# RMSNorm over 16,384 rows: other store sizes, and eight small memsets on VectorE

## Chip, cores and metric

The kernel runs on one core of one Trainium2 chip. The metric is the device time of one execution in microseconds (us); lower is better. The kernel before has a median of 105.37 us over 6 runs (105.22 to 106.1).

## The reference

```python
B, S, D = 512, 32, 640          # x is bf16 [512, 32, 640], g is bf16 [640]
def reference(x, g):
    rms = jnp.sqrt((x * x).mean(axis=-1, keepdims=True) + 1e-6)
    return x / rms * g
```

Each of the 512 x 32 = 16,384 rows of 640 numbers is divided by its root mean square and multiplied by the vector g. The input is 20.97 MB and the output is as large, so 41.9 MB have to move between HBM and SBUF.

## The kernel before

**Layout.** The 16,384 rows are spread over 128 partitions, 128 consecutive rows on each. In what follows "row" means one of these 128 positions: one row is 128 partitions x 640 numbers, or 160 KB. The whole input is kept in SBUF in one tile, `xs`; the result is written over it in place, and stored from there. There are no buffers to wait for on the way in or out.

**Three lists of sizes**, each adding up to 128 rows, cut the work:

- `LOADS = [4, 8, 8, 16, 32, 32, 28]`: seven loads, issued one after the other by ScalarE's queue at the start (L72). The fifth brings rows 36 to 67, the sixth rows 68 to 99, the seventh rows 100 to 127. In each load a partition's rows are one contiguous run.
- `CHUNKS = [2, 2] + [8] * 15 + [4]`: 18 chunks of compute. They end after rows 2, 4, 12, 20, 28, 36, 44 and so on up to 124 and 128.
- `STORES = [28, 24, 24, 24, 8, 8, 8, 4]`: eight stores, issued by SyncE (SP, L139). A store is put into SP's program as soon as all its rows belong to finished chunks, and it waits for VectorE's write of the last of its rows.

**One chunk.** TensorE copies each row of the chunk into PSUM by a multiplication with the identity (`ident`, L108), in two pieces of 512 and 128 columns. ScalarE squares it there and sums it up (L110), one row at a time, into `ms`. (The first chunk of two rows does this on VectorE instead, L99.) ScalarE then takes the square root for the chunk (L119, `rstd`). VectorE multiplies the chunk by g (`times_g`, L124, into `y`), takes the reciprocal (L128), and multiplies each row of `y` by its own factor, one instruction per row, into `xs` (`finish`, L130).

**The order.** The order on PE, VectorE, SP and GpSimd is that in which the code stands (a manual schedule). The loop is pipelined by one chunk: `times_g` of chunk c comes ahead of `finish` of chunk c-1. So VectorE needs the rows of a chunk, loaded, before it finishes the chunk before it; and SP issues a store only after `finish`.

At the start VectorE sets two constants: `ones1` (L64), used to broadcast g over the partitions, and `eps_sb` (L66), which ScalarE's square roots use. After them VectorE's next instruction is the first row's sum of squares (L99), which needs the first load.

Of the kernel before, what the change touches and what calls it, by code (L numbers as in the profile page):

```python
# [1 line left out]

# [5 lines left out]

EPS = 1e-6

LOADS = [4, 8, 8, 16, 32, 32, 28]
CHUNKS = [2, 2] + [8] * 15 + [4]
STORES = [28, 24, 24, 24, 8, 8, 8, 4]


@with_exitstack
def kernel(
    ctx: ExitStack,
    tc: tile.TileContext,
    x: bass.AP,  # L20
    g: bass.AP,
    out: bass.AP,
):
    nc = tc.nc
    P = nc.NUM_PARTITIONS
    ALU = mybir.AluOpType
    ACT = mybir.ActivationFunctionType
    ENG = mybir.EngineType
    f32 = mybir.dt.float32
    bf16 = mybir.dt.bfloat16  # L30

    xf = x.flatten_outer_dims()
    of = out.flatten_outer_dims()
    N, D = xf.shape
    assert N % P == 0
    R = N // P
    assert sum(LOADS) == sum(CHUNKS) == sum(STORES) == R
    JM = max(CHUNKS)

    x_v = xf.rearrange("(p r) d -> p r d", p=P)  # L40
    o_v = of.rearrange("(p r) d -> p r d", p=P)

    consts = ctx.enter_context(tc.tile_pool(name="consts", bufs=1))
    ypool = ctx.enter_context(tc.tile_pool(name="ypool", bufs=3))
    junk = ctx.enter_context(tc.tile_pool(name="junk", bufs=2))
    small = ctx.enter_context(tc.tile_pool(name="small", bufs=4))
    xps = ctx.enter_context(tc.tile_pool(name="xps", bufs=3, space=bass.MemoryType.PSUM))
    mps = ctx.enter_context(tc.tile_pool(name="mps", bufs=2, space=bass.MemoryType.PSUM))

    inv_sqrt_d = 1.0 / float(D) ** 0.5  # L50
    inv_d = 1.0 / float(D)

    ctx.enter_context(tc.manual_schedule(engines={ENG.PE, ENG.DVE, ENG.SP, ENG.Pool}))

    xs = consts.tile([P, R, D], xf.dtype, name="xs")
    g1 = consts.tile([1, D], g.dtype, name="g1")
    g_row = bass.AP(tensor=g.tensor, offset=g.offset, ap=[[0, 1], g.ap[-1]])
    nc.sync.dma_start(out=g1[:], in_=g_row)

    ident = consts.tile([P, P], bf16, name="ident")  # L60
    make_identity(nc, ident)

    ones1 = consts.tile([1, P], bf16, name="ones1")
    nc.vector.memset(ones1[:], 1.0)  # L64
    eps_sb = consts.tile([P, 1], f32, name="eps_sb")
    nc.vector.memset(eps_sb[:], EPS)  # L66
    warm = consts.tile([P, 1], f32, name="warm")

    r = 0
    last = None  # L70
    for i, n in enumerate(LOADS):
        ld = nc.scalar.dma_start(out=xs[:, r:r + n, :], in_=x_v[:, r:r + n, :])  # L72
        r += n
        if i == 1:
            ld = nc.scalar.activation(out=warm[:], in_=eps_sb[:], func=ACT.Sqrt,  # L75
                                      bias=eps_sb[:], scale=1.0)
        if last is not None:
            tc.add_manual_dep(ld.ins, last.ins.name,
                              mybir.DependencyInfo(mybir.DependencyClass.NoSync,
                                                   mybir.DependencyReason.DATA),  # L80
                              reason="order on ScalarE's queue")
        last = ld

    g_sb = consts.tile([P, D], g.dtype, name="g_sb")
    gp = xps.tile([P, D], f32, name="xp")
    for lo, hi in ((0, 512), (512, D)):
        nc.tensor.matmul(out=gp[:, lo:hi], lhsT=ones1[:], rhs=g1[:, lo:hi], start=True, stop=True)  # L87
    nc.scalar.copy(out=g_sb[:], in_=gp[:])  # L88

    def g_bcast(J):  # L90
        return bass.AP(tensor=g_sb.tensor, offset=g_sb.offset,
                       ap=[list(g_sb.ap[0]), [0, J], list(g_sb.ap[-1])])

    def sumsq(c, a, J):
        if c == 0:
            ms = small.tile([P, JM], f32, name="ms0")
            for j in range(J):
                jd = junk.tile([P, D], bf16, name="junk_d")
                nc.vector.scalar_tensor_tensor(  # L99
                    out=jd[:], in0=xs[:, a + j, :], scalar=inv_d, in1=xs[:, a + j, :],  # L100
                    op0=ALU.mult, op1=ALU.mult, accum_out=ms[:, j:j + 1])
            return ms
        ms = mps.tile([P, JM], f32, name="ms")
        before = []
        for j in range(J):
            xp = xps.tile([P, D], f32, name="xp")
            for lo, hi in ((0, 512), (512, D)):
                nc.tensor.matmul(out=xp[:, lo:hi], lhsT=ident[:], rhs=xs[:, a + j, lo:hi],  # L108
                                 start=True, stop=True)
            sq = nc.scalar.activation(out=xp[:], in_=xp[:], func=ACT.Square, scale=inv_sqrt_d,  # L110
                                      accum_out=ms[:, j:j + 1])
            for b in before:
                tc.declare_no_dep(sq.ins, b.ins, reason="disjoint columns")
            before.append(sq)
        return ms

    def rms(ms, J):
        r = small.tile([P, JM], f32, name="rstd")
        nc.scalar.activation(out=r[:, :J], in_=ms[:, :J], func=ACT.Sqrt, bias=eps_sb[:], scale=1.0)  # L119
        return r  # L120

    def times_g(a, J):
        y = ypool.tile([P, JM, D], bf16, name="y")
        nc.vector.tensor_tensor(out=y[:, :J, :], in0=xs[:, a:a + J, :], in1=g_bcast(J), op=ALU.mult)  # L124
        return y

    def finish(a, J, y, r):
        nc.vector.reciprocal(out=r[:, :J], in_=r[:, :J])  # L128
        for j in range(J):
            nc.vector.tensor_scalar_mul(out=xs[:, a + j, :], in0=y[:, j, :], scalar1=r[:, j:j + 1])  # L130

    stores = list(STORES)
    stored = 0

    def store_up_to(done):
        nonlocal stored
        while stores and stored + stores[0] <= done:
            n = stores.pop(0)
            nc.sync.dma_start(out=o_v[:, stored:stored + n, :], in_=xs[:, stored:stored + n, :])  # L139
            stored += n  # L140

    prev = None
    a = 0
    for c, J in enumerate(CHUNKS):
        ms = sumsq(c, a, J)
        y = times_g(a, J)
        r = rms(ms, J)
        if prev is not None:
            finish(*prev)
            store_up_to(prev[0] + prev[1])  # L150
        prev = (a, J, y, r)
        a += J
    finish(*prev)
    store_up_to(R)
    assert not stores


# [1 line left out]
_INS = ['x', 'g']  # L159
_OUTS = [((512, 32, 640), 'bfloat16')]  # L160


# [23 lines left out]
```

## Time and profile before

| | |
|---|---|
| median of 6 runs | 105.37 us (105.22 to 106.1) |
| the profiled execution's own time | 106.03 us |
| its span, first to last instruction | 104.3 us |
| VectorE busy | 87.4 us (84% of the span) |
| ScalarE busy | 88.7 us (85%) |
| TensorE matmuls | 57.3 us (55%) |
| DMA, loads (q10) and stores (q1) | 20.97 MB each, 48.5% and 47.0% of the 16 engines' span |
| issue of the eight stores by SP | from 28.87 to 95.70 us |

All times of views are counted from the start of the span. The 1.7 us between span and time lie around it. The page has a table of 40 slices of the span, here 2.6 us each; a 9 in it says that the engine was busy for 90% of the slice or more. The DMA row is the mean over the 16 DMA engines. The loads go through queue q10 (issued by ScalarE) and the stores through queue q1 (issued by SP); both use the same 16 engines. Instruction fetches show as queues of their own (q8 and q14). In a window's DMA view, a packet counts to the window in which it starts, with all its bytes and time, so a share can be above 100%.

### The profile page before, as it was taken

The numbers are of one execution on the slowest core, as the hardware profiler recorded it, in microseconds if no ns is written. First come the engines' busy times: TensorE is split into PE (matmuls) and PEld (weight loads), VectorE is DVE, ScalarE is ACT, GpSimd is POOL, SyncE is SP. The second block draws the span as 40 slices with busy tenths as digits, with TensorE's granted clock in tenths as the row PEclk, the third lists the DMA queues.
The fourth block names the chain that finished last, engine by engine and source line by source line (L and its number), as shares of the span: only waits on it lengthen the run. The fifth ranks groups of instructions, "written<-read, shape, count | busy, mean of one in ns | idle before, by whom it ended". The sixth has DMA issues, their size and how long they took to land.

```text
span 104.3 us, 1146 instructions
## 1 busy us (share of the span) xinstructions
PE 57.3 (55%) x254; PEld 24.8 (24%) x254; DVE 87.4 (84%) x170; ACT 88.7 (85%) x273; POOL 0.7 (1%) x6
## 2 busy tenths in 40 slices
PE   1238986656666656666656666656666565610000
PEld 0004332222222222222222222222222222200000
DVE  0199999999979999999999999999999999786000
ACT  3457999999999999999999999999999999990000
POOL 2000000000000000000000000000000000000000
PEclk9999999999999999999999999999999999975555
DMA  3999999989979899999999999999999999999970
GB/s 55 409 420 483 401 456 542 393 361 506 471 299 373 334 461 450 442 456 444 413 443 430 422 409 420 409 416 495 413 389 475 431 389 436 385 424 436 416 295 16
DMA packets 2168, 42.01 MB, mean 403 GB/s; under 512 B 241, under 2 KB 242, under 8 KB 498
## 3 DMA queue, kind: packets, MB, share of 16 engines
q10 hardware_dynamic: 1008, 20.97, 48.5%
q1 hardware_dynamic: 1154, 20.97, 47.0%
q8 instruction: 2, 0.03, 0.1%
q14 instruction: 4, 0.03, 0.1%
HBM read 20.97 MB, written 20.97 MB: 402 GB/s over the span
## 4 chain that ended last, share of the span: by engine, by line
ACT 64%; issue 15%; DMA 7%; DVE 3%; PE 1%; ACTq 0%; DVEq 0%
ACT xp L110 62%; DMA xs<-in_x_dram 7%; DVE xs L130 3%; ACT rstd L119 2%; PE xp L108 1%; ACTq L72 0%; DVEq L181 0%; DVE rstd L128 0%; DVEq L130 0%; ACTq L110 0%
## 5 line engine op out<-in xcount | busy, mean ns | idle before, releaser
L110 ACT ACTIVATE xp<-xp 128x640 f32<-128x640 f32 x126 | 85.7, 1203 | 0.7 <-PE xp L108 0.7
L110 ACT ACTIVATION_READ_ACCUMULATOR xp<-xp 128x1 f32 x126 | 76.3, 674 | 0.0
L108 PE MATMUL xp<-xs,ident 128*128 128x512 bf16 x252 | 56.7, 311 | 32.1 <-ACT xp L110 27.8
L124 DVE TENSOR_TENSOR y<-xs,g_sb 128x5120 bf16<-128x5120 bf16 (+2 forms) x18 | 45.3, 2521 | 0.6 <-DMA xs<-in_x_dram 0.6
L130 DVE TENSOR_SCALAR xs<-y,rstd 128x640 bf16<-128x640 bf16 x128 | 39.5, 381 | 1.9
L108 PEld LDWEIGHTS <-ident 128*128 128x128 bf16 x252 | 24.6, 99 | 64.4 <-issue 47.3
L119 ACT ACTIVATE rstd<-ms,eps_sb 128x8 f32<-128x8 f32 (+2 forms) x17 | 11.9, 702 | 0.0
L99 DVE SCALAR_TENSOR_TENSOR junk_d<-xs 128x640 bf16<-128x640 bf16 x2 | 1.6, 822 | 3.9 <-DMA xs<-in_x_dram 3.9
L128 DVE RECIPROCAL rstd<-rstd 128x8 f32<-128x8 f32 (+2 forms) x18 | 3.4, 191 | 1.1 <-ACT rstd L119 1.0
L75 ACT ACT_TABLE_LOAD x1 | 1.3, 1283 | 1.6 <-PEq L170 1.6
L87 PE MATMUL xp<-g_76,ones_83 1*128 1x512 bf16 (+1 forms) x2 | 0.7, 442 | 2.3 <-DMA g_76<-in_g_dram 2.3
L88 ACT CAST g_sb<-xp 128x640 bf16<-128x640 f32 x1 | 0.7, 692 | 1.3 <-issue 1.3
L119 ACT ACTIVATE rstd<-ms_101,eps_sb 128x2 f32<-128x2 f32 x1 | 0.3, 297 | 1.3 <-DVE junk_d L99 1.3
L64 DVE MEMSET ones_83<- 1x128 bf16 x1 | 0.2, 165 | 0.8 <-PEq L170 0.8
L87 PEld LDWEIGHTS <-ones_83 1*128 1x128 bf16 x2 | 0.2, 99 | 2.2 <-issue 1.1
L75 ACT ACTIVATE warm<-eps_sb 128x1 f32<-128x1 f32 x1 | 0.3, 294 | 0.0
masks.py:199 POOL TENSOR_SCALAR_AFFINE_SELECT ident<-ident 128x128 bf16<-128x128 bf16 x1 | 0.3, 292 | 0.1
masks.py:197 POOL MEMSET ident<- 128x128 bf16 x1 | 0.2, 204 | 0.3 <-POOLq L170 0.3
L99 DVE DVE_READ_ACCUMULATOR junk_d<-xs 128x1 f32 x2 | 0.2, 80 | 0.0
L170 POOL MEMSET const-bfloat16-1.0<- 128x1 bf16 x1 | 0.1, 102 | 0.0
L170 POOL MEMSET const-uint8-127<- 128x1 uint8 x1 | 0.1, 102 | 0.0
L170 POOL MEMSET const-float32-0.0<- 128x1 f32 x1 | 0.1, 98 | 0.2 <-issue 0.2
(2 smaller groups left out, 0.2 us busy)
## 6 DMA issues: line engine op xcount, KB each, us to landing
out_dram<-xs SPq DMA_DIRECT2D x3, 3840.0 KB, 17.8
xs<-in_x_dram ACTq DMA_DIRECT2D x2, 5120.0 KB, 36.9
xs<-in_x_dram ACTq DMA_DIRECT2D x1, 4480.0 KB, 67.0
out_dram<-xs SPq DMA_DIRECT2D x1, 4480.0 KB, 29.8
out_dram<-xs SPq DMA_DIRECT2D x3, 1280.0 KB, 9.5
xs<-in_x_dram ACTq DMA_DIRECT2D x2, 1280.0 KB, 8.1
xs<-in_x_dram ACTq DMA_DIRECT2D x1, 2560.0 KB, 15.0
xs<-in_x_dram ACTq DMA_DIRECT2D x1, 640.0 KB, 4.1
```

The source lines that it names most:

```text
L64: nc.vector.memset(ones1[:], 1.0)
L75: ld = nc.scalar.activation(out=warm[:], in_=eps_sb[:], func=ACT.Sqrt, bias=eps_sb[:], scale=1.0)
L87: nc.tensor.matmul(out=gp[:, lo:hi], lhsT=ones1[:], rhs=g1[:, lo:hi], start=True, stop=True)
L88: nc.scalar.copy(out=g_sb[:], in_=gp[:])
L99: nc.vector.scalar_tensor_tensor(out=jd[:], in0=xs[:, a + j, :], scalar=inv_d, in1=xs[:, a + j, :], op0=ALU.mult, op1=ALU.mult, accum_out= ...
L108: nc.tensor.matmul(out=xp[:, lo:hi], lhsT=ident[:], rhs=xs[:, a + j, lo:hi], start=True, stop=True)
L110: sq = nc.scalar.activation(out=xp[:], in_=xp[:], func=ACT.Square, scale=inv_sqrt_d, accum_out=ms[:, j:j + 1])
L119: nc.scalar.activation(out=r[:, :J], in_=ms[:, :J], func=ACT.Sqrt, bias=eps_sb[:], scale=1.0)
L124: nc.vector.tensor_tensor(out=y[:, :J, :], in0=xs[:, a:a + J, :], in1=g_bcast(J), op=ALU.mult)
L128: nc.vector.reciprocal(out=r[:, :J], in_=r[:, :J])
L130: nc.vector.tensor_scalar_mul(out=xs[:, a + j, :], in0=y[:, j, :], scalar1=r[:, j:j + 1])
L170: nc = _bacc.Bacc("TRN2", target_bir_lowering=False, num_devices=1)
```

## The change

The stores get other sizes. The first has 16 rows instead of 28; the three of 24 rows stay, but each begins 12 rows earlier; the rest is cut as 16, 12, 8 and 4 rows instead of 8, 8, 8 and 4. The number of stores stays at eight. Besides, VectorE sets the eight elements of a small new tile, `pad`, one by one, after `eps_sb`. Nothing reads `pad`.

```diff
 LOADS = [4, 8, 8, 16, 32, 32, 28]
 CHUNKS = [2, 2] + [8] * 15 + [4]
-STORES = [28, 24, 24, 24, 8, 8, 8, 4]
+STORES = [16, 24, 24, 24, 16, 12, 8, 4]
...
     eps_sb = consts.tile([P, 1], f32, name="eps_sb")
     nc.vector.memset(eps_sb[:], EPS)
+    pad = consts.tile([1, 8], f32, name="pad")
+    for k in range(8):
+        nc.vector.memset(pad[:, k:k + 1], 0.0)
     warm = consts.tile([P, 1], f32, name="warm")
```

The stores so end after rows 16, 40, 64, 88, 104, 116, 124 and 128, where before they ended after rows 28, 52, 76, 100, 108, 116, 124 and 128. The first five of the new ends lie in the middle of a chunk, after its fourth row. The order of the instructions on PE, ScalarE and GpSimd stays the same, and on VectorE it is the same but for the eight memsets.

## The prediction

> **What bounds the kernel now.** I read the slices of the page first, then the queues, then the chain.
>
> ```profile
> span 104.3 us, 1146 instructions
> ...
> DVE  0199999999979999999999999999999999786000
> ACT  3457999999999999999999999999999999990000
> ...
> DMA  3999999989979899999999999999999999999970
> ...
> q10 hardware_dynamic: 1008, 20.97, 48.5%
> q1 hardware_dynamic: 1154, 20.97, 47.0%
> ...
> ACT 64%; issue 15%; DMA 7%; DVE 3%; PE 1%; ACTq 0%; DVEq 0%
> ```
>
> The chain puts 64% on ScalarE, but ScalarE and VectorE stop about 10 us before the end, and the DMA row stays at 9 until slice 38. The loads (q10) and stores (q1) together occupy the 16 DMA engines for 48.5 + 47.0 = 95.5% of the span, 99.6 us. Little is left but the start, where the first bytes move at about 1.75 us, and the tail. Is work queued when the last store is issued? The DMA view of 94 to 97 us shows KB and the time from issue to landing:
>
> ```profile
> out_dram<-xs SPq DMA_DIRECT2D x1, 1280.0 KB, 7.4
> out_dram<-xs SPq DMA_DIRECT2D x1, 640.0 KB, 7.4
> ```
>
> VectorE writes its last row at 95.66 and the last store (4 rows, 640 KB) is issued at 95.70, yet it lands 7.4 us later, at 103.1. The first load has the same size and lands in 4.1 us. So the last store stands in a queue: **the end is set by the DMA engines emptying their queue**, not by compute. The windows of 5 us agree: the DMA share is 0.94 to 1.07 in every one from 35 to 100 us, at 402 to 461 GB/s.
>
> Compute depends on DMA at one visible place (VectorE's timeline):
>
> ```profile
> 20.94 2.46 DVE L130 TENSOR_SCALAR xs<-y,rstd 128x640 bf16<-128x640 bf16 x8
> 23.32 2.81 DVE L124 TENSOR_TENSOR y<-xs,g_sb 128x5120 bf16<-128x5120 bf16 x1
> ...
> 29.43 2.82 DVE L124 TENSOR_TENSOR y<-xs,g_sb 128x5120 bf16<-128x5120 bf16 x1 [0.59 <-DMA xs<-in_x_dram]
> ...
> 94.39 1.27 DVE L130 TENSOR_SCALAR xs<-y,rstd 128x640 bf16<-128x640 bf16 x4
> ```
>
> At 29.43 VectorE waits 0.59 us for the load of rows 36 to 67; that load lands just in time, and the first store was issued at 28.87. Afterwards VectorE has no recorded wait until 91.43 (0.99 us, for ScalarE), so a delay at 29.4 goes through to its end.
>
> **How two queues share an engine.** The DMA views of 29 to 32, 32 to 35 and 60 to 65 us (packets, MB, share):
>
> ```profile
> q10 hardware_dynamic: 32, 1.31, 131.6%
> ...
> q10 hardware_dynamic: 10, 0.41, 35.1%
> q1 hardware_dynamic: 12, 0.43, 33.1%
> ...
> q10 hardware_dynamic: 32, 1.15, 53.0%
> q1 hardware_dynamic: 32, 0.98, 45.6%
> ```
>
> From 60 to 65 the packets are one to one: 32 load packets of 28 rows (36 KB) against 32 store packets of 24 rows (31 KB). A store with shorter rows per partition therefore takes a smaller share. From 29 to 32, just after the first store's issue, no store packet starts: 32 load packets, two per engine, still go first. In windows of half a microsecond the first store packets start at 33.5, although the load packets before them started by 32.0 and last 1.5 us (32 packets on 16 engines in 3 us): I take 0.8 us as lost in the change-over.
>
> **The Trainium skill.** "DMA: Bandwidth & Descriptors", section "Queues, rings and completion order", says that each engine goes round-robin between its queues, packet by packet; the 32 to 32 agrees. The same page, "Why a DMA increments its semaphore by 16 and not by 1": a transfer counts as landed only when all its engines have finished, so the slowest engine decides; the tail below agrees. "Runtime: NRT & Kernel Launch", section "Instruction fetch mechanics": engines fetch instructions in blocks by DMA; the trace shows six such packets within the span, four of 0.01 MB (q14, at 23, 39, 52 and 80 us) and two of 0.02 MB (q8, at 40 and 81 us).
>
> **The change, part by part.**
>
> *Eight memsets.* VectorE's program gets eight 1x1 memsets after L66. The nearest row is the 128x1 memset at 0.06 us: 8 x 0.06 = 0.5 us, from 1.0 to 1.5. VectorE then idles until 4.90, waiting for the first load (3.90 us), so there are 3.4 us of cover; `eps_sb`, which ScalarE and PE await, is written before them. I cost them at nothing. What they may move is an instruction fetch: 8 instructions further on, VectorE fetches its next block earlier. One 0.01 MB packet takes 0.3 us of one engine (q14 at 23 us: 1.9% of 16 us). A q14 packet also shows just after the span (at 104.6 us); if it is VectorE's, it would move ahead of the end. I bound all this at -0.6 to +0.5 us and take 0.
>
> *Store sizes.* Before: after rows 28, 52, 76, 100, 108, 116, 124, 128. After: 16, 40, 64, 88, 104, 116, 124, 128. Still eight stores, the same bytes and packets, and SP has nothing else to issue. In the built program each store waits for VectorE's write of its own last row; five now end in the middle of a chunk of 8, at its fourth row. L130 takes 1.27 us for four rows (last row of the timeline), so the first is issued at 20.94 + 1.27 = **22.2** instead of 28.87, the next at 39.2, 55.4, 71.6 and 82.5. The last three (88.96, 94.15, 95.7) stay, but for any delay of compute.
>
> *Bytes.* An earlier store doesn't make a full DMA empty sooner. Load-only time (437 GB/s from 26 to 29 us) is exchanged for mixed (418 to 446 in the windows from 50 to 70) and store-only (424 from 70 to 75). 6.6 us at 437 are 2.9 MB; at 424 they take 6.8 us: **+0.2** at most. Small packets don't show: 90 to 95 us runs 218 packets at 418 GB/s.
>
> *The new stall.* At 22.2 the load of rows 36 to 67 isn't finished. One packet per engine starts in 22 to 23; the remaining three start at about 23.6, 25.1 and 26.6. As before, two go ahead of the store; then the 0.8 us change-over, a store packet of 16 rows (20 KB, half of 1.5 = 0.76 us), and the last load packet. That delays the load by 0.8 + 0.76 = 1.6 us, and by 2.3 where two store packets get in on a late engine. The load lands at 31.0 to 31.7, and **PE, ScalarE and VectorE from row 36 on slip by 1.6 to 2.3 us; I take 1.9**. Low bound 0.8 (one packet, no change-over loss), high 3.9 (four packets and the loss). The later loads come earlier: up to about 46 us the store has one third of the share instead of nearly half. The load of rows 68 to 99, which PE awaits at 50.79 (0.17 us), lands by my count near 47.5; it is no second stall.
>
> *What hides it.* VectorE ends at 95.66 + 1.9 = 97.6. Is a store still queued whenever the next one is issued? Issue plus landing before: row 108 at 95.5, 116 at 89.07 + 9.5 = 98.6, 124 at 94.15 + 7.4 = 101.6. Total DMA progress stays the same, so the store of rows 116 to 123, issued at 94.15 + 1.9 = 96.05, reaches the slowest engine's queue, allowing 1 us from issue to first packet (first load: 0.74 to 1.75), at 97.05, still 1.5 us ahead of 98.6. For the last store the margin is 101.6 - (97.6 + 1.0) = 3.0. So **compute may slip by about 1.9 + 1.5 = 3.4 us before the slowest engine starves**. The slip is hidden; faster engines may idle half a microsecond or so.
>
> Sum: 0 + 0.2 + 0 = +0.2 us on the span of 104.3, which with 1.7 us around it is the profiled 106.03. The profiled execution is 0.7 above the median of 105.37. Fetches have an even chance to fall better or worse; with half of the possible gain from the moved fetch I predict **105.3**. For the likeliest case alone I give 104.9 to 105.9. Half a per cent, 0.53 us, is about what a measurement can tell here from no change.
>
> **Rivals.**
>
> *Faster: the DMA engines finish more evenly.* The windows of half a microsecond from 100.5 show shares of 42, 37, 22, 5 and 3%: most engines are done, a few work on until 102.8. The sum is 1.09 x 0.5 = 0.55 us per engine, so a level finish would be near 101.1. The late compute sets a floor: 12 rows (1.97 MB at 420 GB/s, 4.7 us) from 97.05 end at 101.7, against 102.8: up to 1.1 us, or 104.3. Moving VectorE's fetch could give part of it. Against it: nothing in the change levels engines on purpose. Chance 0.27.
>
> *Slower: the stall of rows 36 to 67 outgrows the queue.* If the store gets in at once and takes two packets per turn, four load packets wait 4 x 1.5 + 0.8 = 6.8 us; beyond 3.4 us every microsecond counts. A slip of 5 us costs 1.6 (107.0), 6.8 costs 3.4 (108.8). For it: 28 was the size at which the first store just missed this load. Against: two load packets per engine went ahead at 29 us, and 16-row packets are the smallest of the early stores. With a fetch falling on the slowest engine as the smaller case (+0.3 to 0.9), chance 0.33.
>
> *No effect within 0.5%:* 0.40, the forecast. The memsets' program says what it does, so I leave no chance for an absent change.
>
> **The range.** 104.4 to 107.2 takes in the level finish (104.3 almost), the fetch on either side and a slip of about 5 us; stalls beyond that are left out.
>
> **What would show it.** Right: first store issued near 22.2; VectorE's wait at row 36 of 2 to 3 us in place of 0.59; its last row near 97.6; the last store landing in about 5.5 us instead of 7.4; DMA share near 1 up to 98. Wrong: a last store landing in some 4 us with idle DMA ahead of it (starved), a second stall near 51, or an end moved by over 0.5 us with the queue still full.

## The result, and the profile after

The changed kernel is slower. Its median is 106.56 us (105.51 to 106.89, 20 runs) against 105.65 us (105.19 to 106.53, 40 runs) for the kernel before on the same chip; the ratio is **1.0065, 95% interval 1.0045 to 1.0086**. I had forecast 105.3 us and no change. The profiled execution took 106.75 us, with a span of 104.9.

The page of the changed kernel (lines are now three higher: L124 is L127, L130 is L133):

```profile
span 104.9 us, 1155 instructions
...
DVE  1199999999905999999999999999999999989500
ACT  3457999999961999999999999999999999998000
...
PEclk9999999999975599999999999999999999999755
DMA  3999999979969898979999999999999959979892
...
q10 hardware_dynamic: 1008, 20.97, 48.1%
q1 hardware_dynamic: 1154, 20.97, 46.9%
...
ACT 40%; DMA 29%; DVE 14%; issue 9%; ACTq 1%; PE 0%; DVEq 0%
```

Two things are new. VectorE has a hole in slices 11 and 12 (28.9 to 34.1 us), and ScalarE one at the same place. And the DMA row, which was 9 from slice 14 to 37 before, falls to 5 in slice 32, 83.9 to 86.6 us (the first slice is 0). The chain's DMA share rose from 7% to 29%: the chain now passes through a load. (PEclk, the TensorE clock that was granted, falls to half after the hole; a run below has the loss without that.) VectorE's timeline shows which load it is:

```profile
20.91 2.46 DVE L133 TENSOR_SCALAR xs<-y,rstd 128x640 bf16<-128x640 bf16 x8
...
32.77 2.82 DVE L127 TENSOR_TENSOR y<-xs,g_sb 128x5120 bf16<-128x5120 bf16 x1 [3.95 <-DMA xs<-in_x_dram]
...
97.42 1.27 DVE L133 TENSOR_SCALAR xs<-y,rstd 128x640 bf16<-128x640 bf16 x4
```

The product of rows 36 to 43 starts at 32.77 instead of 29.43: a **slip of 3.34 us**. It goes through to VectorE's last row, which ends at 98.69 instead of 95.66. The windows late in the run, with each engine's busy time and then the TensorE clock, the DMA share and the GB/s:

```profile
85.00:87.50 2.50, 1.63 (x8) 0.67 (x8) 2.50 (x9) 2.50 (x11) 0.00 (x0) 1.00 0.41 162
...
92.50:95.00 2.50, 1.56 (x8) 0.57 (x6) 1.89 (x4) 2.50 (x10) 0.00 (x0) 1.00 0.73 305
```

Before, the DMA engines were full in both:

```profile
85.00:87.50 2.50, 1.47 (x7) 0.67 (x7) 2.39 (x6) 2.50 (x12) 0.00 (x0) 1.00 1.05 455
92.50:95.00 2.50, 0.00 (x0) 0.00 (x0) 2.39 (x10) 1.14 (x5) 0.00 (x0) 0.50 0.99 418
```

In the changed kernel they have run out of work twice, while compute is still busy. The last two stores, with their KB and the time from issue to landing, are:

```profile
out_dram<-xs SPq DMA_DIRECT2D x1, 1280.0 KB, 5.3
out_dram<-xs SPq DMA_DIRECT2D x1, 640.0 KB, 5.4
```

5.4 us in place of 7.4: hardly anything stands ahead of them but each other. The last store is issued just after VectorE's last row and lands near 104.1, against 103.1 before.

### The profile page after: what moved, and what is told of

Its sections match the earlier page's. It is cut to its first block, busy times and chain, and to the rows that moved or that the text cites. A ratio compares the mean times of both kernels' runs of the same rounds, so it can differ in the third digit from the quotient of the medians.

```text
span 104.9 us, 1155 instructions
## 1 busy us (share of the span) xinstructions
PE 58.2 (55%) x254; PEld 25.1 (24%) x254; DVE 87.6 (83%) x178; ACT 88.8 (85%) x273; POOL 0.7 (1%) x6
## 3 DMA queue, kind: packets, MB, share of 16 engines
q10 hardware_dynamic: 1008, 20.97, 48.1%
q1 hardware_dynamic: 1154, 20.97, 46.9%
## 4 chain that ended last, share of the span: by engine, by line
ACT 40%; DMA 29%; DVE 14%; issue 9%; ACTq 1%; PE 0%; DVEq 0%
ACT xp L113 39%; DMA xs<-in_x_dram 29%; DVE xs L133 8%; DVE y L127 5%; ACT rstd L122 1%; ACTq L75 1%; ACT L78 0%; PE xp L111 0%; DVE rstd L131 0%; DVEq L184 0%; DVEq L133 0%; ACTq L122 0%
## 5 line engine op out<-in xcount | busy, mean ns | idle before, releaser
L111 PE MATMUL xp<-xs,ident 128*128 128x512 bf16 x252 | 57.5, 318 | 34.2 <-ACT xp L113 26.6
L113 ACT ACTIVATION_READ_ACCUMULATOR xp<-xp 128x1 f32 x126 | 70.3, 610 | 0.0
L127 DVE TENSOR_TENSOR y<-xs,g_sb 128x5120 bf16<-128x5120 bf16 (+2 forms) x18 | 45.3, 2521 | 4.0 <-DMA xs<-in_x_dram 4.0
L133 DVE TENSOR_SCALAR xs<-y,rstd 128x640 bf16<-128x640 bf16 x128 | 39.6, 380 | 2.0
L122 ACT ACTIVATE rstd<-ms,eps_sb 128x8 f32<-128x8 f32 (+2 forms) x17 | 10.9, 643 | 0.0
```

## The experiments

Every ratio is to the kernel before, timed beside it, with its 95% interval. The theory tested is the *stall theory*: the early first store delays the load of rows 36 to 67, compute slips, and the stores are issued too late to keep the DMA engines busy. Its rivals are that the memsets move instruction fetches to a bad place, that the late cuts leave the queue too empty, and that the early store itself costs DMA time.

**One part alone: the memsets.** The kernel before with `pad` and its eight memsets.

> The kernel before with the eight memsets alone. Stall theory (the early store delays the load of rows 36 to 67, and compute slips by 3.3 us): no stall, VectorE waits about 0.6 us at row 36, its last row near 95.7, time within 0.3% of before. Fetch theory (the memsets move VectorE's instruction fetches onto a DMA engine that then ends last): slower by 0.5% or more with the stores unchanged. A third outcome: the time from the last landing to the end of the span falls from 1.15 to about 0.8 us, as in the changed kernel, because the fetch at 104.6 us moves ahead of the end; then 0.3% faster.

Measured: 0.9977 (0.9954 to 1.0001). The stall is absent (the wait at row 36 is 0.69 us). The third outcome came in at the end of the span; the time's interval just takes in no change. SP's waits near the end, of the kernel before and then of this one (engine, line, what it waited for, us in total, times, longest):

```profile
SPq L181 <- PEq L181: 0.9, 2, 0.7
```

```profile
SPq L184 <- PEq L184: 0.6, 2, 0.4
```

The closing barrier, at which all engines wait for each other, is 0.3 us shorter. The trace names PE's sequencer as the releaser, but the instruction that moves is VectorE's drain, one of that barrier: before, it starts 0.50 us after its release, here 0.11 us. VectorE's last instruction fetch, which before came after the end (104.6 us), is now at 96.1. The fetch theory of a loss falls.

**The other part alone: the store sizes**, without memsets.

```diff
-STORES = [28, 24, 24, 24, 8, 8, 8, 4]
+STORES = [16, 24, 24, 24, 16, 12, 8, 4]
```

> The changed kernel without the eight memsets. Stall theory: the whole loss stays, ratio 1.005 to 1.010, VectorE waits about 4 us at row 36, last store issued near 99.05. Fetch theory: the loss is gone, ratio within 0.3% of 1 with the same stall.

Measured: 1.0037 (1.0013 to 1.0062), with a wait of 3.35 us at row 36. The loss is there without the memsets. It is somewhat smaller than expected, and so is the stall, 3.35 us where some 4 were expected.

**The early issue undone, all else kept.** The changed kernel, but SP's first store also waits for VectorE's write of row 27 (the edit is shortened here).

```diff
     def store_up_to(done, m=None):
+        if done < 28:
+            return
...
+            if stored == 0:
+                tc.add_manual_dep(st.ins, m.ins.name, Sync, DATA)   # m: last row of finish
```

> The changed kernel, its sizes and memsets kept, but the first store of 16 rows is held until VectorE has finished row 28, as in the kernel before. Stall theory: issue near 28.9, the load of rows 36 to 67 lands near 29.4, the wait at row 36 is 0.6 us, VectorE ends near 95.7 and the time is that of the kernel before within 0.3%. Theory of the late cuts (the stores that end at 88, 104 and 116 leave the queue too empty): slower by 0.4% or more, since these stay.

Measured: **0.9933 (0.9915 to 0.9951), faster than both kernels.** The first store goes at 29.14. VectorE's timeline, its wait at row 36 and its last rows:

```profile
29.72 2.83 DVE L127 TENSOR_TENSOR y<-xs,g_sb 128x5120 bf16<-128x5120 bf16 x1 [0.61 <-DMA xs<-in_x_dram]
...
94.67 1.27 DVE L133 TENSOR_SCALAR xs<-y,rstd 128x640 bf16<-128x640 bf16 x4
```

The stall is back to 0.61 us, VectorE ends at 95.94, and the DMA shares from 85 to 87.5 and from 92.5 to 95 us are 1.00 and 0.95: the engines no longer run dry. So the early issue alone costs 1.0065 / 0.9933 = 1.013, about 1.4 us, and the rest of the change is a gain. The theory of the late cuts as a loss falls: they are all in this kernel.

**The slip without the early store.** The kernel before, with useless work on VectorE ahead of the product of rows 36 to 43, nine multiplications and, in a later run, five.

```diff
         ms = sumsq(c, a, J)
+        if a == 36:
+            for k in range(9):          # later run: range(5)
+                jd = junk.tile([P, D], bf16, name="junk_d")
+                nc.vector.tensor_tensor(out=jd[:], in0=g_sb[:], in1=g_sb[:], op=ALU.mult)
         y = times_g(a, J)
```

> The kernel before with nine useless multiplications of 128x640 on VectorE ahead of the g product of rows 36 to 43, some 3.3 us; stores and loads are those of before, the first store goes at 28.87. Stall theory in its simple form (any slip of compute of about 3.3 us starves the DMA queues near the end): VectorE ends near 98.5 to 99, DMA share below 0.95 in some window from 85 to 98, slower by 0.4 to 0.9%. Theory of the late cuts: the slip is harmless with the stores of before, within 0.3%.

Measured: 1.0073 (1.0051 to 1.0095). VectorE's timeline around the added work, and the window in which the DMA share falls:

```profile
29.06 3.70 DVE L149 TENSOR_TENSOR junk_d<-g_sb 128x640 bf16<-128x640 bf16 x9
32.68 2.81 DVE L124 TENSOR_TENSOR y<-xs,g_sb 128x5120 bf16<-128x5120 bf16 x1
```

```profile
80.00:82.50 2.50, 1.62 (x8) 0.76 (x8) 2.50 (x8) 2.50 (x10) 0.00 (x0) 1.00 0.27 108
...
90.00:92.50 2.50, 1.33 (x7) 0.48 (x5) 2.39 (x9) 2.50 (x12) 0.00 (x0) 1.00 0.76 324
```

Loads and first store are those of before; only VectorE is late, by 3.2 us, and the loss is of the size of the change's. VectorE ends at 98.2. The engines run dry from 80 to 82.5, ahead of the store of rows 76 to 99, and that with the late cuts of before. The slip by itself is enough, without an early store. The granted clock stays at 1.00 from 30 to 40 us here, where in the changed kernel it was 0.50 from 32.5 to 35, so the loss doesn't need it; nor does VectorE's slip grow after it in the changed kernel (3.3 us at row 36, 3.0 at the end).

> The kernel before with five useless multiplications on VectorE ahead of the g product of rows 36 to 43, some 1.9 us, after which VectorE may catch up 1 us at its wait for ScalarE near 91. Stall theory with its threshold: a slip of about 2 us is hidden by the full queue, ratio 0.996 to 1.001 (the fetch after the end is moved too). If every slip costs in proportion, then two thirds of the nine multiplications' loss, ratio above 1.003.

Measured: 0.9979 (0.9960 to 0.9998). The product of rows 36 to 43 starts at 30.82, 1.4 us late, but VectorE has caught up most of that by its end, 96.07; the share from 80 to 82.5 is 1.05. A slip of 0.4 us at VectorE's end is hidden: the loss has a threshold, but this run doesn't show where.

**The changed kernel again.**

> The changed kernel once more, beside the others of this call. Stall theory: ratio 1.004 to 1.008 again, the wait at row 36 between 3.3 and 4 us.

Measured: 1.0097 (1.0064 to 1.0129), with a wait of 4.24 us at row 36. Both are above what was expected; the loss is there again.

**The early store kept, the load in its way cut.**

```diff
-LOADS = [4, 8, 8, 16, 32, 32, 28]
+LOADS = [4, 8, 8, 16, 16, 32, 44]
```

> The changed kernel with LOADS = [4, 8, 8, 16, 16, 32, 44]: the load that starts at row 36 ends at row 51 instead of 67 and lands before the first store's packets. The early store at 22.2 stays. Stall theory: no wait of over 0.5 us at row 36, none of over 0.5 us at row 52 (needed near 40), VectorE ends near 95.7 and the time is like that of the held store, ratio 0.990 to 0.998. Theory that the early store itself costs DMA time whatever it delays: still slower than before.

Measured: 1.0288 (1.0254 to 1.0323); the expectation missed. The stall at row 36 is gone, but two others take its place (VectorE's timeline):

```profile
42.42 2.83 DVE L127 TENSOR_TENSOR y<-xs,g_sb 128x5120 bf16<-128x5120 bf16 x1 [2.58 <-DMA xs<-in_x_dram]
...
67.44 2.83 DVE L127 TENSOR_TENSOR y<-xs,g_sb 128x5120 bf16<-128x5120 bf16 x1 [3.29 <-DMA xs<-in_x_dram]
...
99.41 1.27 DVE L133 TENSOR_SCALAR xs<-y,rstd 128x640 bf16<-128x640 bf16 x4
```

The loads that begin at rows 52 and 84 come too late. As a test of an early store without a stall it failed, and it can't tell whether the early store itself costs DMA time. The pages can: loads and stores take 48.1 + 46.9 = 95.0% of 104.9 us in the changed kernel, 99.7 us, and 99.6 before. As a third size of slip the run is of use: VectorE ends at 100.7, and the last store again lands 5.4 us after its issue.

**The late cuts without the early start**, with the memsets.

```diff
-STORES = [16, 24, 24, 24, 16, 12, 8, 4]
+STORES = [28, 24, 24, 12, 16, 12, 8, 4]
```

> The first three stores of before (28, 24, 24), then 12, 16, 12, 8, 4, with the memsets: the late part of the change without the early start. Theory of the late cuts as a gain (they are why the held store was 0.67% faster than before): ratio near 0.993 like the held store. If the gain of the held store came from its smaller first store, this one is like the memsets alone, ratio near 0.998. If the late cuts cost: above 1.002.

Measured: 0.9965 (0.9950 to 0.9979), between the two expected values and not to be told from the memsets alone (0.9977).

**The held first store with the late ends of before.** The hold is the one shown above.

```diff
-STORES = [16, 24, 24, 24, 16, 12, 8, 4]
+STORES = [16, 36, 24, 24, 8, 8, 8, 4]
```

> The held first store of 16 rows with the later ends of before: STORES = [16, 36, 24, 24, 8, 8, 8, 4], first store held until row 28, memsets kept. If the held store's gain beyond the memsets (0.9933 against 0.9977) comes from the smaller first store, which leaves the DMA engines less apart, ratio near 0.993 and last landings of the engines at most 2.2 us apart. If it comes from the late cuts, ratio near 0.998 and 2.4 to 2.8 us apart.

Measured: 0.9952 (0.9930 to 0.9974). It lies between the two expected values; the interval takes in 0.993 and ends just short of 0.998. The engines' last landings are 2.0 us apart, which was the sign of the smaller first store; but with a first store of 24 rows, below, they are 1.9 apart without a gain beyond the memsets, so this sign decides nothing.

**The held first store without memsets.**

> The held store without the eight memsets. If the memsets are worth the 0.32 us of the tail (1.15 to 0.83 us from the last landing to the end): ratio 0.996 to 0.997, tail 1.15 us, VectorE's fetch after the end. If they are worth nothing there: 0.993 with the tail unchanged at 0.83.

Measured: 0.9960 (0.9939 to 0.9981). SP's barrier wait is 0.9 us again and VectorE's last fetch is back after the end.

**Other first sizes**, with the memsets: 20 and 24 rows.

```diff
-STORES = [16, 24, 24, 24, 16, 12, 8, 4]
+STORES = [20, 24, 24, 24, 12, 12, 8, 4]     # second kernel: [24, 24, 24, 24, 8, 12, 8, 4]
```

> STORES = [20, 24, 24, 24, 12, 12, 8, 4] with the memsets: the first store goes near 23.4. Stall theory, packet by packet: on the early engines the last packet of the load of rows 36 to 67 is already committed, only the late engines wait for one store packet; the load lands near 31, VectorE slips by 1.3 to 2 us, which is hidden: ratio 0.993 to 1.000. If the stall is not a matter of packets still to come but of the mixed rate, nearly the loss of the 16-row store: ratio above 1.003.

> STORES = [24, 24, 24, 24, 8, 12, 8, 4] with the memsets: the first store goes near 27.7, when the last packets of the load of rows 36 to 67 have started. Stall theory: landing near 29.4, wait at row 36 0.5 to 1 us, ratio 0.992 to 0.998.

Measured: 1.0035 (1.0010 to 1.0061) for 20, the second of its two outcomes, and 0.9982 (0.9964 to 1.0000) for 24, a hair above what was expected. VectorE's wait at row 36 with 20 rows, and then with 24:

```profile
31.75 2.83 DVE L127 TENSOR_TENSOR y<-xs,g_sb 128x5120 bf16<-128x5120 bf16 x1 [3.14 <-DMA xs<-in_x_dram]
```

```profile
29.14 2.82 DVE L127 TENSOR_TENSOR y<-xs,g_sb 128x5120 bf16<-128x5120 bf16 x1 [0.46 <-DMA xs<-in_x_dram]
```

24 rows, issued at 27.5, are as harmless as 28. 20 rows, issued at 23.2, still cost 2.3 us at row 36, more than I expected; and a VectorE end of 97.7 is already too late.

## Why the prediction was wrong

**What held.** The first store was issued at 22.2, as worked out:

```profile
22.21 76.84 SPq L142 DMA_DIRECT2D out_dram<-xs  x8
```

The stall came at row 36 and nowhere else. The memsets hid in VectorE's idle start. The queue does hide a short slip. What I had as the slower rival, the stall outgrowing the queue, is what happened in kind.

Two things came true by luck. The load of rows 68 to 99 brought no second stall, but it landed at 51.8 and not near 47.5; compute was 3 us late and did not need it yet. And the last store landed in 5.4 us, near the 5.5 that I gave as a sign of being right, though with idle DMA ahead of it.

**The first step that failed: the size of the slip**, 1.9 us in the sum, 3.3 measured. The stores' and loads' packets in the DMA views of 26 to 28 and 28 to 30 us of the changed kernel:

```profile
q10 hardware_dynamic: 16, 0.66, 111.6%
q1 hardware_dynamic: 14, 0.29, 33.3%
...
q10 hardware_dynamic: 3, 0.12, 21.9%
q1 hardware_dynamic: 7, 0.14, 16.6%
```

16 engines in 2 us make 32 us of engine time. 16 load packets took 111.6% of it, 35.7 us, or 2.2 us each instead of 1.5. Three more start between 28 and 30 and last 7.0 / 3 = 2.3 us. My own line of 29 to 32 us before had shown it: 131.6% of 48 us for 32 packets is 2.0 us each, and I read 1.5 us and a pause. I had counted this loss of 0.8 us once per engine. It fell on thirteen engines once or a little more; on the other three, two store packets came ahead and two load packets were slowed, by 1.0 to 1.4 us together.

A third term I had put at nothing. Behind its share of a load each engine moves one packet of 4 bytes, and only then has the share landed. In the views of 30 to 32 and 32 to 34 us they are the packets under 512 B:

```profile
DMA packets 51, 1.04 MB, mean 522 GB/s; under 512 B 13, under 2 KB 13, under 8 KB 13
...
DMA packets 33, 0.90 MB, mean 451 GB/s; under 512 B 3, under 2 KB 3, under 8 KB 3
```

Before, this packet moved as soon as the engine's data were done. In the changed kernel one more store packet of 0.76 us went ahead of it on every engine: thirteen engines had their data by 30.3 us, moved the small packet by 31.1 and landed at 31.1 to 31.4; the other three had their data at 31.6, moved it at 32.3 to 32.4 and landed at 32.7.

So the thirteen were delayed by about 2.4 us, not 1.6; that they landed inside my 31.0 to 31.7 is luck, because I had added the delay to the slowest engine's landing. I had priced the three at 0.8 + 2 x 0.76 = 2.3 us; it was 3 x 0.76 for store packets and 1.0 to 1.4 for slower load packets, 3.3 to 3.6. The slowest case, not the middle one, was the number to take, and even that was 1 us short. The slower packets and the store packet ahead of the small one also made me expect too little of the 20-row store; there no engine let two store packets ahead of the load's data.

**The second step: the threshold of 3.4 us.** It says how far compute may slip before the queue is empty. I took the margin at the last two stores only, from the landings of before, that is from the slowest engine, and supposed that DMA progress up to there stays the same. In the changed kernel the queue first ran dry at the store of rows 88 to 103: its issue slipped from my 82.5 to 86.0, when most engines had already finished the store before it (share 0.41 from 85 to 87.5). After that even the slowest engine has little in stock: it finishes the store of rows 88 to 103 at 94.8, 2.2 us after the next one's issue at 92.6, and the store of rows 104 to 115 at 99.4, 2.1 us after the next issue. Before, the last figure was 98.55 - 94.23 = 4.3 us. The profiles give the threshold:

| kernel | VectorE's last row ends | last store, issue to landing | ratio |
|---|---|---|---|
| before | 95.7 | 7.4 us | 1 |
| five multiplications | 96.1 | 6.7 us | 0.9979 |
| first store 20 rows | 97.7 | 5.4 us | 1.0035 |
| sizes without memsets | 97.9 | 5.5 us | 1.0037 |
| nine multiplications | 98.2 | 5.9 us | 1.0073 |
| changed | 98.7 | 5.4 us | 1.0065 |
| changed, again | 99.0 | 5.4 us | 1.0097 |
| split load | 100.7 | 5.4 us | 1.0288 |

Once the queue is dry, the landing follows VectorE's end by some 5.4 us (by 5.9 with the store sizes of before, in the run with nine multiplications). Before, it came at 103.1, so by this estimate the slip begins to count at 103.1 - 5.4 = 97.7, **about 2 us after VectorE's end of before and not 3.4**. These are single profiles, and the edge is good to about half a us: the profiled execution of before took 0.4 us more than its median, that of the 20-row kernel, just at the edge here but slower, 0.2 us less. By themselves the runs show that a slip of 0.4 us at VectorE's end is hidden and one of 2.0 is not.

With my own estimate of 1.9 us the change would have stood just at that edge; the real slip of 3.0 us at VectorE's end is 1.0 beyond it, and the last landing moved by 1.0, from 103.1 to 104.1. It took both errors: 3.3 us lie under my threshold, and 1.9 us about at the real one.

**The terms on the other side.** I gave the memsets a bound of -0.6 to +0.5 us and took half of the possible gain. Every kernel profiled with five or more added VectorE instructions, memsets or multiplications, has the fetch ahead of the end and the 0.3 us shorter barrier; the three without (before, sizes alone, held without memsets) have neither. The sign and place were right: 0.3 us, though the timing of the memsets alone (0.9977, up to 1.0001) does not prove it to half a per cent. How the two hang together is not shown: in the kernel before, the drain is over at 104.0 us, ahead of the fetch's packet at 104.6, so it doesn't wait for that packet. The sizes, which I costed at +0.2 us, are a gain once the store is held: 0.9960 without memsets. Together: early issue +1.3%, memsets -0.3%, sizes -0.4%, about the +0.65% measured; the first was worked out from that very number, so this divides it up and proves nothing.

**What stays open.** Whether the 0.4% comes from the smaller first store or the late cuts: 0.9933, 0.9952 and 0.9965 have overlapping intervals. And whether the memsets lengthen the stall: it was 3.95 and 4.24 us with them and 3.35 without, one profile each; the ratios, 1.0065 and 1.0097 with them and 1.0037 without, go against their gain at the barrier. And why load packets took longer beside the first store packets.

## What to carry to other kernels

Here, where DMA is full from end to end, an earlier store brought nothing, but it took turns from a load that compute was about to need. Hold such a store until that load's last packets are under way: issue at 27.5 us was late enough and 23.2 was not. Here that took one dependency, and with the new sizes and the memsets the time was 0.67% less than before. When you ask whether a slip is hidden, check the queue at every store from the slip to the end and on the engines that finish first, not only at the last store on the slowest one. And where a transfer ends with its slowest engine, price the delay of that engine, with the small packet behind its data.

## What was not expected of the hardware

A load's packets of 40 KB, 1.5 us each when alone, took 2.2 to 2.3 us each beside the first packets of a store on the other queue. Later in the mixed stage that was not so: from 60 to 65 us the kernel before shows 32 load packets of 36 KB at 53.0% of 80 us of engine time, 1.3 us each. The 4-byte packet behind a load's data moved only after one more store packet, 0.76 us later, on all sixteen engines. And five to nine more instructions on VectorE, useless ones, shortened the closing barrier by 0.3 us.
